# Four shared PSUM rooms, one copy per gather, swaps in eight pieces and a new hand-written order in a gated mix of two long convolutions

## The chip, the cores and the metric

The kernel runs on one core of a Trainium2 chip. The metric is the device time of one execution in microseconds (us). The engines of a core work side by side and each takes its own instructions strictly in their order: TensorE (PE, with its weight loads as PEld), VectorE (DVE), ScalarE (ACT), GpSimd (POOL) and SyncE (SP). DMA transfers are issued by SP, ACT and POOL and run beside the engines. Matmuls write to PSUM, whose eight banks hold 2 KB in each of 128 partitions; a matmul result stays there until DVE or ACT has copied or used it ("evicted").

## The reference

A gate between two long convolutions over L = 2048 positions of D = 448 channels.

```python
# A: diagonal state-space model, kernel K generated from 256 modes per channel
P = exp((dt * (A_re + 1j A_im))[:, :, None] * l)          # D x N x L
K = einsum("dn,dnl,dn->dl", C, P, dt * B).real
a = irfft(rfft(pad(u)) * rfft(pad(K)))[:L] + u * Dskip
# B: shift convolution of four taps, product, long convolution, product
ks = sum(k_padded[t:t+S] * shift_k[:, 3-t] for t in range(4))
kv = ks * v
b = u * (irfft(rfft(pad(kv)) * rfft(pad(ssm_k)))[:S] + kv * ssm_D)
g = sigmoid((u * gate_w).sum(-1, keepdims=True))          # one value for each position
out = g * a + (1 - g) * b                                  # bf16
```

## The kernel before, in words

The 448 channels are four groups of 112 on the partitions, and they are worked through in NQG = 4 steps of NC = 28 channels per group, for B and for A each. A long convolution is a transform done by matmuls. `spread` brings the columns of an input to a tile zs (128 x 32 x 112) through PSUM tiles ps_c. `transform` multiplies it in place, eight of 32 slices to a PSUM tile (the trace calls the tile ps). A second copy with the two halves of the partitions exchanged, zsS, is made by DMA (`swapped`, lines 764 to 768). `products` (line 399) multiplies zs and zsS by the transformed kernel of the convolution. `stage_a` (PSUM ps_a, result U) and `stage_b` (PSUM ps_b) go back, and the epilogues multiply, add and store.

Convolution A needs its kernel K first. `Tables` computes exponentials and sines on ACT (tiles ET, ks_mag, with DVE's phases ks_ph), in four chunks, one for two of the NBLK = 8 blocks of 14 channels per group. `KGen.block` (line 464) builds two tables of powers on DVE (kg_TQ for two blocks, kg_TP for one; kg_P are partial products) and sums over the modes with 448 matmuls into PSUM tile pk, which one copy brings to kg_S. `KGen.gather` (line 511) picks rows with small matmuls into ps_g, a PSUM tile of one bank for each half, and each half is copied to KT (kg_KT) by a strided copy of 448. `block` (line 891) then spreads KT with weights WcK into the tile zsK of the step: for blocks 0 to 5 in four pieces of 4, 4, 4 and 2 columns through one-bank tiles (name ps_g, seen as ps_c in the trace), for the last two in pieces of 8 and 6 through the two-bank rooms.

PSUM is divided at lines 722 and 723: a pool `psum` of three rooms of two banks, in which all of the transforms take turns, and a pool `psk` of single buffers, one bank for pk (line 885) and one for ps_g (line 516 and the spreads of blocks 0 to 5). A matmul that needs a room waits until the room's last content has been evicted.

Evictions go to ACT (`evac`, line 728), or to ACT and DVE by turns (`evac_two`) in the last block.

The front of the run loads the taps shift_k by four small transfers on ACT's queue (line 781), makes from them a diagonal weight tile (in `front`), transposes k by DMA, and convolves it on PE in eight pieces ps_v, which DVE multiplies into vt. Beside this the tables of the first chunk, the weights and the first spreads are made.

The order of the work: the kernel is first recorded, call by call, by the class `Order` (lines 137 to 155). `issue` then replays the calls by the list ORDER (lines 42 to 112: ranges of call numbers), and makes each engine's order the order of that list. So all instructions carry line 149 in the profile, and tiles tell them apart. The steps run

```python
seq = [("B", 0), ("B", 1), ("A", 0), ("B", 2), ("A", 1), None, ("A", 2), ("B", 3)]
for j in range(NBLK - 1):
    step(seq[j], seq[j + 1], j)
```

Each `step` (line 955) holds the spreads and transforms of the next convolution, the stages back of the current one and block j. ORDER interleaves these freely. Behind the loop come the eighth block, the last halves of A's fourth step, the mix and the stores.

Of the kernel before, what the change touches and what calls it, by code (L numbers as in the profile page):

```python
# [136 lines left out]
class Order:  # L137

    def __init__(self, tc):
        self.tc, self.calls = tc, []  # L140
        for e in ("vector", "scalar", "tensor", "gpsimd", "sync"):
            setattr(self, e, Listed(self.calls, getattr(tc.nc, e)))

    def issue(self):
        last, done = {}, 0
        for run in ORDER.split():
# [914 lines left out]
```

## Time and profile before

| | |
|---|---|
| median of 3 runs | 265.6 us (265.38 to 266.52) |
| the profiled execution | 266.88 us |
| its span in the trace | 264.8 us |
| DVE busy | 243.4 us, 506 instructions |
| ACT busy | 226.8 us, 375 instructions |
| PE busy | 213.7 us, 5786 matmuls |
| mean granted TensorE clock | 0.942 of full speed |
| swaps | 16 transfers of 448 KB, 4.4 us from issue to landing |

The page shows busy time by engine, then 40 slices of the span in tenths of busy time, then the chain of work that ended last, then groups of instructions (out<-in, shape, count, busy us, mean ns of one, and the idle time of their engine before them with what ended it). Other views cut the span into windows, or list an engine's instructions in time.

### The profile page before, as it was taken

How to read it: one execution, taken by the hardware profiler on the slowest of the kernel's cores; microseconds unless marked ns; L12 is line 12 of the kernel's file. 1: busy time of each engine (PE TensorE's matmuls, PEld its weight loads, DVE VectorE, ACT ScalarE, POOL GpSimd, SP SyncE). 2: the span in 40 equal slices, each digit the busy share in tenths (PEclk: the TensorE clock that was granted, in tenths of full speed). 3: DMA queues.
4: the chain of work that ended last, by engine and by line, in shares of the span. 5: the costliest groups of instructions: out<-in, count | busy, mean ns of one | idle time of the engine just before them, and what ended most of it. 6: DMA issues, size and time to landing. Idle time of an engine off the chain costs nothing.

```text
span 264.8 us, 12775 instructions
## 1 busy us (share of the span) xinstructions
PE 213.7 (81%) x5786; PEld 194.2 (73%) x5786; DVE 243.4 (92%) x506; ACT 226.8 (86%) x375; POOL 11.8 (4%) x46
## 2 busy tenths in 40 slices
PE   1611849799799999999899898899979998989820
PEld 1501739788688889889788788889969888979720
DVE  6599999899999999999989999989999999989950
ACT  2998789997999999999999999999999999485400
POOL 8000000000000100010100100001000100000000
PEclk9999979999999869999999999999986999999955
DMA  7999669952833702045626230423240360600087
GB/s 153 218 189 192 104 134 203 176 83 32 158 72 72 159 4 57 4 80 119 109 51 141 41 92 2 90 56 73 50 97 2 72 144 2 144 5 2 2 158 122
DMA packets 57077, 24.27 MB, mean 92 GB/s; under 512 B 52032, under 2 KB 54720, under 8 KB 57024
## 3 DMA queue, kind: packets, MB, share of 16 engines
q1 hardware_dynamic: 50752, 19.34, 38.9%
q0 software_dynamic: 1008, 3.21, 6.6%
q10 hardware_dynamic: 5264, 0.92, 2.1%
q8 instruction: 45, 0.74, 1.2%
q14 instruction: 8, 0.07, 0.1%
HBM read 7.95 MB, written 2.87 MB: 41 GB/s over the span
## 4 chain that ended last, share of the span: by engine, by line
DVE 37%; ACT 35%; PE 16%; DMA 4%; issue 3%; SPq 0%; ACTq 0%; DVEq 0%
ACT zs L149 12%; ACT zsK L149 7%; ACT ET L149 6%; DVE kg_P L149 5%; PE ps_v L149 4%; ACT U L149 4%; DVE kg_TQ L149 3%; PE ps_b L149 3%; DVE kg_TP L149 3%; DVE ET L149 3%; PE ps_c L149 3%; DVE zsS L149 3%; DVE vt L149 3%; DVE zs L149 3%; DVE sb_G L149 2%
## 5 line engine op out<-in xcount | busy, mean ns | idle before, releaser
L149 ACT CAST zs<-ps 128x896 bf16<-128x896 f32 x48 | 43.8, 944 | 1.9 <-PE ps L149 1.9
L149 ACT CAST zs<-ps_c 128x1024 bf16<-128x1024 f32 (+1 forms) x48 | 44.0, 976 | 0.5 <-PE ps_c L149 0.4
L149 PEld LDWEIGHTS <-front 128*32 128x32 bf16 (+1 forms) x496 | 19.9, 160 | 27.8 <-issue 17.3
L149 PE MATMUL pk<-kg_TP,kg_TQ 128*32 128x32 bf16 x1792 | 35.4, 241 | 0.9 <-issue 0.7
L149 PEld LDWEIGHTS <-kg_TQ 128*32 128x32 bf16 x1792 | 31.8, 160 | 3.5 <-issue 0.9
L149 PEld LDWEIGHTS <-s_W 128*128 128x128 bf16 x544 | 27.9, 98 | 7.9 <-issue 4.5
L149 PE MATMUL ps_a<-sa_R,zs 128*128 128x128 bf16 x224 | 32.0, 231 | 1.2 <-DVE zs L149 0.7
L149 PE MATMUL ps_b<-U,sb_G 128*128 128x28 bf16 x1024 | 30.8, 178 | 2.6 <-DVE U L149 1.2
L149 ACT CAST U<-ps_a 128x1024 bf16<-128x1024 f32 (+1 forms) x30 | 27.9, 962 | 5.4 <-PE ps_a L149 5.4
L149 PEld LDWEIGHTS <-sb_G 128*128 128x128 bf16 x1024 | 28.7, 98 | 4.7 <-issue 1.9
L149 PE MATMUL ps_v<-front 128*32 128x336 bf16 (+3 forms) x448 | 17.3, 319 | 17.1 <-DVE sb_offs L149 6.9
L149 PE MATMUL ps_a<-sa_R,zsS 128*128 128x128 bf16 x224 | 31.1, 227 | 0.0
L149 PEld LDWEIGHTS <-zs 128*128 128x128 bf16 x224 | 29.0, 150 | 1.9 <-DVE zs L149 0.8
L149 PEld LDWEIGHTS <-zsS 128*128 128x128 bf16 x224 | 29.4, 152 | 0.7 <-DVE zsS L149 0.4
L149 PE MATMUL ps<-zs,s_W 128*128 128x112 bf16 x384 | 27.1, 215 | 3.0 <-ACT zs L149 2.5
L149 DVE TENSOR_TENSOR kg_TP<-kg_TP,ET 128x1792 bf16<-128x1792 bf16 x23 | 24.7, 1083 | 0.5 <-ACT ET L149 0.5
L149 DVE TENSOR_TENSOR kg_TQ<-kg_TQ,ET 128x896 bf16<-128x896 bf16 (+1 forms) x36 | 24.6, 720 | 0.0
L149 ACT ACTIVATE ET<-ks_ph 128x448 bf16<-128x448 int16 x40 | 22.6, 596 | 1.8 <-DVE ks_ph L149 1.7
L149 DVE TENSOR_TENSOR kg_P<-kg_TP,ET 128x1792 bf16<-128x1792 bf16 (+1 forms) x25 | 23.3, 934 | 0.1
L149 ACT ACT_TABLE_LOAD x15 | 19.2, 1283 | 2.0 <-issue 1.8
L149 PE MATMUL ps_c<-Wc,uu 128*64 128x128 bf16 x224 | 18.7, 290 | 0.4 <-ACT zsK L149 0.2
L149 PE MATMUL ps_c<-Wc,vt 128*64 128x128 bf16 x224 | 17.2, 289 | 1.2 <-ACT zs L149 1.2
(101 smaller groups left out, 424.7 us busy)
## 6 DMA issues: line engine op xcount, KB each, us to landing
zsS<-zs SPq DMA_DIRECT2D x16, 448.0 KB, 4.4
kg_TP<-kg_P POOLq DMA_DIRECT2D x7, 448.0 KB, 4.4
vt<-in_B_v_dram SPq DMA_DIRECT2D x4, 448.0 KB, 7.5
skraw<-in_B_ssm_k_dram SPq DMA_DIRECT2D x16, 112.0 KB, 3.4
uu<-in_A_u_dram SPq DMA_DIRECT2D x4, 448.0 KB, 7.1
ks_xf<-xfd SPq DMA_DIRECT2D x3, 336.0 KB, 3.1
out_dram<-vt SPq DMA_DIRECT2D x8, 112.0 KB, 4.4
out_dram<-vt ACTq DMA_DIRECT2D x8, 112.0 KB, 4.6
```

Source lines behind the costliest of these rows:

```text
L149: ins = f(*args, **kw)
```

## The change

- PSUM: `psum` has four rooms of two banks, and `psk` is gone. pk and ps_g are now tiles of the shared rooms. ps_g uses both banks of a room, one for each half.
- The gather's two copies of 448 to KT become one of 896 whose writes are contiguous.
- The spread of KT always goes in pieces of 8 and 6 columns through the shared rooms.
- A swap is eight transfers of 64 partitions by 8 of the 32 slices (112 KB) instead of two of 64 partitions by 32 (448 KB).
- The taps are loaded by two transfers (three groups, then one) instead of four.
- ORDER is new. A list TURNED names 16 recorded copies that change their engine, from ACT to DVE or from DVE to ACT.

The order changes which call stands where on each engine: both transfers of the taps stand ahead of ACT's first work, on SP the load of A_re comes first and that of C_im behind the first of k's transposes, the loads of vt stand behind all four transposes, and the exponentials and sines of the first chunk stand in longer runs, with 3 table loads on ACT in the front instead of 9. On DVE there are 497 instructions instead of 506, and PE has the same number of matmuls.

```diff
--- before.py
+++ after.py
@@ -40,76 +40,82 @@
 NBH = 1
 
 ORDER = (
-    "1 949 553-554 540-541 538-539 557 555-556 962-963 544 964 545 527 559 2 53 60 529 951 533 528 560 18 966 558 7 "
-    "3 11 10 534 12 6 898 916 8 950 61 548 959 0 22 531 36 31-32 34 887 63-65 4 68 67 15 9 952 66 572-576 542 25 914 "
...
-    "6700 6702 6661 6701 6775 6699 6663 "
+    "975 1 961 525-526 557 551 538 0 955 976 558 536 58 970 561 60 552 966 953 962 562 2-3 563 553 540 539 566-567 "
+    "565 527 963 29 23 554 911 964 24 541 30 33 555 537 542 22 61-62 954 956 531 556 967 957 5 11 544 547 900 59 63 "
...
 )
+
+TURNED = (
+    "62 951 1487 1509 2130 2988 4042 4270 6008 6213 6541 6561 6570 6588 6618 6652 "
+)
+
 
 def entry_of(e):
     return 2 + 3 * Q_LEVELS.index(e) if e in Q_LEVELS else EQ_N + 2 + 3 * P_LEVELS.index(e)
@@ -141,7 +147,13 @@
         for e in ("vector", "scalar", "tensor", "gpsimd", "sync"):
             setattr(self, e, Listed(self.calls, getattr(tc.nc, e)))
 
+    def turn(self):
+        for i in map(int, TURNED.split()):
+            f, args, kw = self.calls[i]
+            self.calls[i] = (self.tc.nc.vector.tensor_copy if f.__name__ == "copy" else self.tc.nc.scalar.copy, args, kw)
+
     def issue(self):
+        self.turn()
         last, done = {}, 0
         for run in ORDER.split():
             a, _, b = run.partition("-")
@@ -405,8 +417,8 @@
 
 class KGen:
 
-    def __init__(self, tc, nc, pool, pk, psk, cons, sel_d, d4, EQ, EP):
-        self.tc, self.nc, self.pk, self.psk = tc, nc, pk, psk
+    def __init__(self, tc, nc, pool, psum, cons, sel_d, d4, EQ, EP):
+        self.tc, self.nc, self.psum = tc, nc, psum
         self.pool, self.cons, self.sel_d, self.d4, self.EQ, self.EP = pool, cons, sel_d, d4, EQ, EP
 
     def mult(self, srcs, r, m):
@@ -492,7 +504,7 @@
         back(8, 16)
         back(0, 8)
         at = (j % 2) * M
-        pt = self.pk[:, 0:448].rearrange("p (n b) -> p n b", b=32)
+        pt = self.psum.tile([P, 2, 512], f32, name="pk", tag="ps")[:, 0, 0:448].rearrange("p (n b) -> p n b", b=32)
         for hw in range(CB):
             for hf in range(2):
                 for c in range(2):
@@ -512,9 +524,9 @@
         nc, cons = self.nc, self.cons
         KT = self.pool.tile([P, CB, 64], bf16, name="kg_KT")
         for r in range(8):
-            if r % 4 == 0:
-                pt = self.psk.tile([P, 512], f32, name="ps_g")
-            o = pt[:, (r % 4) * 112:(r % 4) * 112 + 112].rearrange("p (b n) -> p b n", b=8)
+            if r == 0:
+                pt = self.psum.tile([P, 2, 512], f32, name="ps_g", tag="ps")
+            o = pt[:, r // 4, (r % 4) * 112:(r % 4) * 112 + 112].rearrange("p (b n) -> p b n", b=8)
             jobs = []
             for odd in (range(2) if r == 4 else (None,)):
                 st = 1 if odd is None else 2
@@ -547,8 +559,7 @@
                     jobs[jobs.index(x)] = x + (i == 0, i == len(mine) - 1)
             for a0, out, lhsT, rhs, begin, end in jobs:
                 nc.tensor.matmul(out, lhsT=lhsT, rhs=rhs, start=begin, stop=end, tile_position=(0, 32 * a0))
-            if r % 4 == 3:
-                evac(KT[:].rearrange("p n (b r) -> p n b r", r=8)[:, :, :, r - 3:r + 1], pt[:, 0:448].rearrange("p (r b n) -> p n b r", r=4, b=8), r // 4)
+        evac(KT[:].rearrange("p n (b f r) -> p n b f r", b=8, f=2), pt[:, :, 0:448].rearrange("p f (r b n) -> p n b f r", r=4, b=8))
         return KT
 
 
@@ -719,8 +730,7 @@
     wp = ctx.enter_context(tc.tile_pool(name="wp", bufs=1))
     nat = ctx.enter_context(tc.tile_pool(name="nat", bufs=1))
     qp = ctx.enter_context(tc.tile_pool(name="qp", bufs=NBQ))
-    psum = ctx.enter_context(tc.tile_pool(name="psum", bufs=3, space=PSUM))
-    psk = ctx.enter_context(tc.tile_pool(name="psk", bufs=1, space=PSUM))
+    psum = ctx.enter_context(tc.tile_pool(name="psum", bufs=4, space=PSUM))
     dram = ctx.enter_context(tc.tile_pool(name="dram", bufs=1, space=DRAM))
     kgp = ctx.enter_context(tc.tile_pool(name="kgp", bufs=1))
     xfd = dram.tile([P, NBLK, 3, M], f32, name="xfd")
@@ -763,8 +773,9 @@
 
     def swapped(zs):
         swap = qt([P, 32, 4 * NC], "zsS")
-        for r in range(2):
-            nc.sync.dma_start(swap[64 * r:64 * r + 64], zs[64 - 64 * r:128 - 64 * r])
+        for k in range(0, 32, 8):
+            for r in range(2):
+                nc.sync.dma_start(swap[64 * r:64 * r + 64, k:k + 8], zs[64 - 64 * r:128 - 64 * r, k:k + 8])
         return zs, swap
 
     early = kgp.tile([P, 7168], i32, name="early", tag="kg_TQ")
@@ -778,8 +789,9 @@
     cons.rows()
     wraw = cons.carve(8).bitcast(bf16).rearrange("p (g t) -> p g t", t=4)
     top = lambda g: min(112 * g, 320)
-    for g in range(4):
-        nc.scalar.dma_start(wraw[:, g], B_shift_k[top(g):top(g) + P, :])
+    rows = B_shift_k[0:P, :]
+    nc.scalar.dma_start(wraw[:, 0:3], bass.AP(rows.tensor, rows.offset, [[4, P], [448, 3], [1, 4]]))
+    nc.scalar.dma_start(wraw[:, 3], B_shift_k[top(3):top(3) + P, :])
     nc.gpsimd.memset(kt[:, :, 0:16], 0.0)
     for g in range(4):
         nc.sync.dma_start_transpose(kt[:, g, 16:2064].unsqueeze(1), B_k[0][:, top(g):top(g) + P])
@@ -882,9 +894,8 @@
     dj = cons.carve(32)[0:4]
     nc.gpsimd.iota(dj[:], pattern=[[1, 32]], base=0, channel_multiplier=-8)
     V.tensor_scalar(out=sel_d[:], in0=dj[:], scalar1=0.0, scalar2=None, op0=ALU.is_equal)
-    pk = psk.tile([P, 512], f32, name="pk")
-
-    kg = KGen(tc, nc, kgp, pk, psk, cons, sel_d, d4, EQ, EP)
+
+    kg = KGen(tc, nc, kgp, psum, cons, sel_d, d4, EQ, EP)
     KA = [None] * NQG
     XA = [None] * NQG
 
@@ -899,10 +910,7 @@
         KT = kg.gather(j, S, ev)
         at = (j % 2) * CB
         cols = lambda c: KT[:, c, :]
-        if j >= NBLK - 2:
-            spread(nc, psum, WcK, KA[H], cols, [range(0, 8), range(8, 14)], ev, at=at)
-        else:
-            spread(nc, psk, WcK, KA[H], cols, [range(0, 4), range(4, 8), range(8, 12), range(12, 14)], evac, 4, "ps_g", at)
+        spread(nc, psum, WcK, KA[H], cols, [range(0, 8), range(8, 14)], ev, at=at)
 
     def window(t, b0, n, H):
         return t[:, b0:b0 + n, H * NC:(H + 1) * NC]
```

134 rows, old and new, of the table ORDER are left out of this document.

## The prediction

> **What bounds the kernel now.** The page comes first: the span, busy time by engine, the 40 slices and the chain that ended last.
>
> ```profile
> span 264.8 us, 12775 instructions
> PE 213.7 (81%) x5786; PEld 194.2 (73%) x5786; DVE 243.4 (92%) x506; ACT 226.8 (86%) x375; POOL 11.8 (4%) x46
> ...
> DVE  6599999899999999999989999989999999989950
> ACT  2998789997999999999999999999999999485400
> ...
> DVE 37%; ACT 35%; PE 16%; DMA 4%; issue 3%; SPq 0%; ACTq 0%; DVEq 0%
> ```
>
> VectorE (DVE) is busy for 243.4 of 264.8 us, and its gaps lie in the first three slices and the last two. ScalarE (ACT) is full between. The chain changes between the two and belongs to neither. So the question is not which engine is busiest but in which stage an engine still stands idle. The windows view answers that (the span cut into stretches; for each: length, then busy us of PE, PE's weight loads, DVE, ACT, POOL, the granted clock, the DMA share, GB/s).
>
> ```profile
> 0.00:20.00 20.00, 6.09 (x51) 4.62 (x51) 15.20 (x72) 14.57 (x30) 5.65 (x39) 1.00 1.06 187
> 20.00:40.00 20.00, 9.82 (x229) 8.82 (x233) 19.79 (x58) 15.70 (x22) 0.00 (x0) 0.91 0.84 144
> 40.00:48.00 8.00, 7.06 (x232) 6.69 (x226) 6.77 (x18) 7.91 (x16) 0.00 (x0) 1.00 1.12 191
> 48.00:200.00 152.00, 140.71 (x3767) 127.54 (x3761) 149.29 (x291) 148.65 (x250) 5.31 (x6) 0.97 0.40 78
> 200.00:212.40 12.40, 12.31 (x296) 11.28 (x296) 12.29 (x18) 11.96 (x24) 0.85 (x1) 0.86 0.22 40
> 212.40:255.30 42.90, 37.73 (x1238) 35.30 (x1234) 40.06 (x53) 28.05 (x40) 0.00 (x0) 0.95 0.26 58
> 255.30:264.80 9.50, 0.00 (x0) 0.00 (x0) 0.03 (x1) 0.00 (x0) 0.00 (x0) 0.50 0.86 144
> ```
>
> DVE's idle time is length less busy: 4.80 us before 20, 0.21 to 40, 1.23 to 48, only 2.71 in the 152 us to 200, 0.11 to 212.40. That is 9.06 us ahead of 212.40, and 6.24 of them lie before 48. From 212.40 DVE has 40.06 of 42.90 us to do, PE 37.73. The last 9.50 us are stores, with no engine busy. So three things can shorten this kernel: DVE's waits in the front, DVE's work, and the chain of PE and DVE behind 212.40. PE idles 11.29 us between 48 and 200, ACT 3.35: PE has a little room there, ACT hardly any.
>
> **The front.** The timeline of DVE (start, length, operation, and in brackets the idle time before it) and of ACT with its DMA issues:
>
> ```profile
> 4.66 0.30 DVE L149 CAST scratch<-scratch 112x4 f32<-112x4 bf16 x1 [0.35 <-ACT scratch L149]
> ...
> 9.32 1.56 DVE L149 TENSOR_TENSOR front<-scratch 128x1344 bf16<-128x1344 bf16 x1 [3.12 <-DMA scratch<-in_B_shift_k_dram]
> ...
> 47.87 1.09 DVE L149 TENSOR_TENSOR vt<-ps_v,vt 128x896 bf16<-128x896 f32 x1 [1.07 <-PE ps_v L149]
> ```
> ```profile
> 4.42 0.20 ACT L149 ACTIVATE scratch<-ldt 112x4 bf16<-112x4 bf16 x1 [1.36 <-DMA ldt<-in_A_log_dt_dram]
> 4.43 1.35 ACTq L149 DMA_DIRECT2D scratch<-in_B_shift_k_dram  x3
> 6.83 0.54 ACT L149 COPY early<-ps_m 128x448 f32<-128x448 f32 x1 [2.20 <-PE ps_m L149]
> ```
>
> Three of the four tap loads are issued at 4.43, behind an exponential that waits until 4.42 for log_dt. DVE then waits 3.12 us for the last to land. In the new order both tap loads stand ahead of the exponential and of the first table load. Their landing should take what the last one takes now: issued near 5.3, used at 9.32, about 4 us. So issued by about 2 they land near 6. The lists also put about 2.5 us more DVE work ahead of that product. I cost the wait at nothing: **−3.1**. Its cover is those 2.5 us; without it up to about 1 us would remain. The small cast moves to ACT: **−0.35**. The eight products vt<-ps_v idle 1.23 us between 40 and 48. With four rooms instead of three, PE can have one more product's matmuls finished: between 0 and −1.23, I take **−0.9**, since most of it sits before the eighth product.
>
> ACT's table loads: 15 become 9; in the front 9 become 3. Rows of the grouping by form (busy us, mean ns of one | idle before):
>
> ```profile
> L149 ACT ACT_TABLE_LOAD x15 | 19.2, 1283 | 2.0 <-issue 1.8
> ...
> L149 ACT CAST zsK<-ps_c 128x512 bf16<-128x512 f32 x18 | 11.6, 647 | 0.6 <-PE ps_b L149 0.4 <-PE ps_c L149 0.2
> ...
> L149 ACT CAST zsK<-ps 128x896 bf16<-128x896 f32 x12 | 11.2, 975 | 0.5 <-PE ps L149 0.5
> ...
> L149 ACT CAST kg_KT<-ps_g 128x448 bf16<-128x448 f32 x15 | 8.4, 559 | 0.6 <-PE ps_g L149 0.4
> ...
> L149 ACT CAST kg_S<-pk 128x448 bf16<-128x448 f32 x8 | 4.4, 545 | 0.0
> ...
> L149 ACT CAST zsK<-ps_c 128x256 bf16<-128x256 f32 x6 | 2.5, 419 | 0.0
> ...
> L149 ACT CAST zsK<-ps_c 128x1024 bf16<-128x1024 f32 x2 | 2.1, 1034 | 0.5 <-PE ps_c L149 0.5
> ...
> L149 DVE CAST U<-ps_a 128x768 bf16<-128x768 f32 x2 | 1.9, 952 | 0.0
> ...
> L149 DVE COPY kg_TP<-ET 128x224 bf16<-128x224 bf16 x8 | 1.7, 212 | 0.2
> ...
> L149 DVE COPY kg_TQ<-ET 128x448 bf16<-128x448 bf16 x4 | 1.1, 272 | 0.3 <-PE pk L149 0.3
> ...
> L149 DVE CAST zsK<-ps_c 128x768 bf16<-128x768 f32 x1 | 0.9, 949 | 0.0
> ...
> L149 ACT CAST zsK<-ps_c 128x768 bf16<-128x768 f32 x1 | 0.8, 826 | 0.0
> ...
> L149 DVE CAST kg_KT<-ps_g 128x448 bf16<-128x448 f32 x1 | 0.6, 623 | 0.6 <-PE ps_g L149 0.6
> ```
>
> Six loads at 1.283 us are 7.7 us of ACT. This is the largest single number in the change, and I count **0** of it. ACT idles 5.43 + 4.30 us before 40 already. In the new lists its first sines of the second chunk stand behind DVE work that ACT reaches earlier than before, so it waits there instead. DVE, not ACT, is the fuller engine up to 48 (41.76 of 48 us against 38.18).
>
> The Trainium skill ("ScalarE: Activation LUTs", section "What ACT_TABLE_LOAD costs") gives about 1283 ns for the load, which is the row's figure, and a drain of about 1380 ns besides; by it the six would be worth 16.0 us of ACT. The count of 0 stays, since ACT's time there is not what ends last.
>
> **The gather and the spread.** Sixteen evictions of kg_KT (8.4 + 0.6 us) become eight on ACT of twice the size. No row has one with that read order; the nearest of its size is zsK<-ps 128x896 at 0.975, so 7.8. The floor is the 0.545 that half the size costs (kg_S), the ceiling two old copies, 1.12. The spread's 28 evictions (11.6 + 2.5 + 2.1 + 0.8 + 0.9 = 17.9) become 8 x 1.034 + 8 x 0.826 = 14.9. On ACT a part of that comes back: two 768 copies of U move to ACT, and 8 small copies turn. In sum ACT does about 5 us less over the whole run, nearly all of it table loads.
>
> DVE loses U 768 (1.9), zsK 768 (0.9), kg_KT (0.6), five kg_TP<-ET (1.06), one kg_TQ<-ET (0.27) and two small copies (0.6): 5.3. It gains one U copy of 512 (about 0.7). Neighbours overlap by some 0.07 us an instruction (about ten of them). That is **−4.0 us of DVE work**: 243.4 to 239.4. But where it falls matters. Counting DVE's listed work ahead of the last kg_TQ product (the one that ends near 212.40), the new order has only **0.5** less. The other 3.5 come behind it, where DVE is not alone in setting the end.
>
> **The end.** Timeline of PE behind the last kg_TQ product:
>
> ```profile
> 216.12 1.21 PE L149 MATMUL pk<-kg_TP,kg_TQ 128*32 128x32 bf16 x64
> 217.25 0.57 PE L149 MATMUL ps<-zsK,s_W 128*128 128x112 bf16 x8
> 217.75 0.73 PE L149 MATMUL pk<-kg_TP,kg_TQ 128*32 128x32 bf16 x32
> ```
>
> Block 7's 448 pk matmuls cannot begin before that product. In the old list transform matmuls ps<-zsK stand between them, eight to each room, 0.50 us for eight (217.25 to 217.75). In the new list 24 of these stand ahead of the first pk matmul that needs the last kg_TQ. PE's work behind that point falls by 3 x 0.50 = 1.5, the matmuls being otherwise the same. PE has 37.73 of 42.90 us there and takes turns with DVE and ACT, so shorter evictions could give more, and an unlucky turn less: between +1 and −4, I take the PE figure, **−1.5**.
>
> **The swaps.** Each swap was two transfers of 64 partitions, 7168 B a row; it becomes eight of 1792 B.
>
> ```profile
> 64.71 1.18 SPq L149 DMA_DIRECT2D zsS<-zs  x2
> ```
> ```profile
> L149 SPq DMA_DIRECT2D zsS<-zs x16: 461/563/2222, 64.7 to 226.0; - x16
> ...
> DMA to landing us min/median/max: 4.0/4.4/6.7
> ```
> ```profile
> 74.80 2.01 DVE L149 TENSOR_TENSOR zsS<-zsS,zs 128x3584 bf16<-128x3584 bf16 x1
> ```
>
> SP issues one in 0.563 us (median), so eight take 4.5 where two took 1.18. If a piece lands 4.4 us after its issue, the swap ends 7 x 0.56 + 4.4 = 8.3 us after its start; now the second piece ends 0.6 + 4.0 to 6.7. So up to 3.7 us later, or about level. Lower than level is possible if a smaller piece lands sooner: the 112 KB stores and loads on the page's list lie beside bigger ones with no clear order, so I leave that at 0. The first swap started at 64.71 and its product at 74.80: 10.1 us, of which 8.3 are used, and the new list lets it start earlier. I take **0**. Behind the pieces on SP stand skraw and ks_xf loads, needed some 10 us later.
>
> **The sum.** −3.1 − 0.35 − 0.9 − 0.5 − 1.5 = −6.35. The small waits between 48 and 212.40 (2.82 in all) I leave where they are. The profiled execution took 266.88 us (span 264.8 and 2.08 around it); it becomes 260.5. The median of the three runs is 265.6, 1.28 below the profiled one, so 259.2.
>
> **The rivals.**
> *Rooms (slower).* kg_S, kg_KT and both spread evictions of a block now hold one of the four shared rooms, and each of the four stands in ACT's full queue. Before, pk and ps_g had a private bank each, and the spreads of six of the eight blocks used the second. If PE stops for each of them, a block costs 0.545 + 0.975 + 1.034 + 0.826 = 3.38 us of PE. PE's idle time, 11.29 us over seven blocks, absorbs 1.6 of it, and the gain of 6.35 another 0.9. So from 2.5 us a block the sign turns; at the full price it is 7 x (3.38 − 1.6) = +12.5: 271.7. For it speaks that ACT stands idle only 3.35 us in that stretch, so that an eviction rarely goes at once. Against it: the rooms become four where there were three, the old private banks were single and made the chain from pk to zsK serial too, and in the rows above little idle time is put down to kg_KT or kg_S (0.6 us for each form at most).
> *Late front.* Another arrival takes the place of the taps: k's transposed loads or the log_dt chain (ACT's 2.20 us wait for ps_m at 6.83). Then 3 of the 4.35 us of the front stay: 262.2, range 262 to 264.5.
> *Pieces late.* A product waits for a swap. The Trainium skill ("DMA: Bandwidth & Descriptors", section "🔬 Bandwidth") asks for transfers of 1 MiB or more and calls those under 64 KB bound by descriptors; 112 KB lies between, so by it the eight pieces are a loss. In this kernel's rows the loss could be 0 to 3.7 us at each of eight swaps, less their slack; if half of them are short of slack by 1.5, +6: 265.2, range 261 to 268.
> *More.* The waits of 2.82 in the middle go too and the end gives 4: 259.2 − 1.3 − 2.5 = 255.4, range 253.5 to 256.5.
> That the eight pieces don't do what they seem to (they still wait for the whole tile, since the products read all of it) is in the sum, at 0.
>
> **How the numbers follow.** Forecast 259.2, own range 256.5 to 262: 0.62, all faster. More: 0.10, faster. Late front: 0.10, of which 0.02 within 0.5%. Rooms: 0.12, of which 0.01 within. Pieces: 0.06, a third to each sign. A measurement of this kernel can tell about 0.5%, 1.3 us, from no change. Faster 0.62 + 0.10 + 0.08 + 0.02 = 0.82, same 0.05, slower 0.13. The range 254.5 to 265 leaves out the rooms case, the dearer half of the pieces and the edge of the best case, 0.19.
>
> **What would show it.** Right: no DVE wait of over 1 us on the taps, under 3 us of DVE idle before the last vt product, nine table loads and ACT idle before 40 not smaller than the 9.7 of now, 239 to 240 us of DVE busy, the last kg_TQ product about 5 us earlier, no DVE wait on a swap. Wrong: PE idle between 48 and 200 over 20 us, put down to ACT's kg_S, kg_KT or zsK (rooms); a DVE wait on zsS's DMA (pieces); a new front wait of 3 us; or a last kg_TQ product that is 5 us earlier while the end is not.

## The result and the profile after

The changed kernel takes 263.12 us (median of 12 runs, 261.74 to 265.33), the kernel before 267.05 on the same chip (12 runs, 265.38 to 268.82): a ratio of 0.985, interval 0.982 to 0.988, or 3.9 us. Run once more beside the variants below, it gave 261.34 us, ratio 0.982 (0.978 to 0.986), or 4.8 us by the ratio. The forecast was 6.35 us less. The profiled execution took 261.79 us, span 259.5. That is 5.1 us below the profiled one of before, and among the fastest of the twelve.

The page of the changed kernel: span, busy time by engine, the 40 slices of VectorE (DVE) and ScalarE (ACT), and the chain.

```profile
span 259.5 us, 12882 instructions
...
PE 211.7 (82%) x5786; PEld 193.9 (75%) x5786; DVE 238.0 (92%) x495; ACT 221.6 (85%) x360; POOL 13.3 (5%) x46
...
DVE  8999999999799989989989999998999999995940
ACT  2899839999999989999989999999999998849400
...
ACT 19%; PE 13%; DVE 9%; DMA 4%; issue 3%; SPq 0%; ACTq 0%; DVEq 0%
```

DVE's first slice went from 6 to 8 and its second from 5 to 9, so the front filled up. In exchange a 7 and four 8s stand in the middle, where there were two 8s and otherwise 9s. To see what that means in time, cut the span at two marks that both kernels have: the end of the last product vt<-ps_v, and the end of the last product kg_TQ<-kg_TQ,ET. The windows of the kernel before (length, then busy us of PE, weight loads, DVE, ACT, POOL, clock, DMA share, GB/s):

```profile
0.00:48.96 48.96, 23.82 (x528) 20.87 (x529) 42.72 (x147) 38.74 (x67) 5.65 (x39) 0.97 0.98 171
48.96:215.48 166.52, 155.10 (x4076) 140.91 (x4076) 163.26 (x312) 163.13 (x277) 6.17 (x7) 0.96 0.39 75
215.48:254.91 39.43, 34.80 (x1182) 32.47 (x1181) 37.08 (x49) 24.96 (x34) 0.00 (x0) 0.95 0.21 48
```

and of the changed one:

```profile
0.00:42.88 42.88, 25.00 (x536) 22.39 (x536) 41.36 (x145) 31.59 (x66) 7.17 (x39) 0.96 0.98 173
42.88:212.55 169.67, 153.95 (x4104) 140.87 (x4100) 162.99 (x308) 165.15 (x264) 6.16 (x7) 0.98 0.44 82
212.55:249.32 36.77, 32.74 (x1152) 30.65 (x1150) 33.21 (x45) 24.82 (x33) 0.00 (x0) 0.95 0.19 40
```

Front −6.08, middle **+3.15**, end −2.66, and the stores behind it +0.29 (10.18 against 9.89): −5.30, which is the difference of the spans. More was won in the front than forecast, and half of it was given back in the middle. In a second profile (after_again) the same stretches take 43.78, 169.16 and 36.44 us. DVE has no more work in the middle (162.99 against 163.26) but waits 6.68 us instead of 3.26. ACT has 2.02 us more work there. None of that is left over from the front, where ACT did 27.7 us besides its table loads, against 27.2 before. By the forms in the stretch, four copies zsK<-ps that stood behind the last kg_TQ product now stand ahead of it (3.6 us), six turned copies came from DVE (2.8 us), and the larger copies of kg_KT and of the spreads save 3.9 us.

DVE's timeline shows the new waits (start, length, operation, idle time before it and what ended it):

```profile
7.63 1.54 DVE L161 TENSOR_TENSOR front<-scratch 128x1344 bf16<-128x1344 bf16 x1
...
68.00 2.02 DVE L161 TENSOR_TENSOR zs<-zs 128x3584 bf16<-128x3584 bf16 x1 [1.49 <-ACT zs L161]
...
91.97 1.09 DVE L161 TENSOR_TENSOR vt<-ps_b,uu 128x896 bf16<-128x896 f32 x1 [1.02 <-PE ps_b L161]
...
114.86 0.62 DVE L161 TENSOR_TENSOR kg_P<-kg_TP,ET 128x896 bf16<-128x896 bf16 x1 [0.98 <-DMA kg_TP<-kg_P]
...
132.66 1.09 DVE L161 TENSOR_TENSOR kg_TP<-kg_TP,ET 128x1792 bf16<-128x1792 bf16 x1 [0.84 <-DMA kg_TP<-kg_P]
...
238.06 0.62 DVE L161 CAST zsK<-ps 128x448 bf16<-128x448 f32 x1 [2.58 <-PE ps L161]
```

The tap wait of 3.12 us at `front` is gone. In its place stand a product that probably waits for a swap (the row at 68.00 names ACT, but the last piece was issued at 65.42 and zs may not be overwritten before it is read), powers that wait for an accumulating transfer, and a product on ps_b that waits for PE; the last row, an eviction, lies in the end. Three different releasers, each about 1 us, speak against one slow thing.

The forms that the change made (busy us, mean ns | idle before):

```profile
L161 ACT ACT_TABLE_LOAD x9 | 11.5, 1283 | 2.4 <-issue 2.3
L161 ACT CAST zsK<-ps_c 128x1024 bf16<-128x1024 f32 x8 | 8.3, 1042 | 0.2 <-PE ps_c L161 0.2
L161 ACT CAST kg_KT<-ps_g 128x896 bf16<-128x896 f32 x8 | 7.5, 942 | 1.4 <-PE ps_g L161 1.2
L161 ACT CAST zsK<-ps_c 128x768 bf16<-128x768 f32 x8 | 6.6, 829 | 0.4 <-PE ps_a L161 0.4
```

### The profile page after: what moved, and what is told of

It is laid out like the page before. It is cut to its first block, busy times and chain, and to the rows that moved or that the text cites. A ratio compares the mean times of both kernels' runs of the same rounds, so it can differ in the third digit from the quotient of the medians.

```text
span 259.5 us, 12882 instructions
## 1 busy us (share of the span) xinstructions
PE 211.7 (82%) x5786; PEld 193.9 (75%) x5786; DVE 238.0 (92%) x495; ACT 221.6 (85%) x360; POOL 13.3 (5%) x46
## 3 DMA queue, kind: packets, MB, share of 16 engines
HBM read 7.95 MB, written 2.87 MB: 42 GB/s over the span
## 5 line engine op out<-in xcount | busy, mean ns | idle before, releaser
L161 PEld LDWEIGHTS <-front 128*32 128x32 bf16 (+1 forms) x496 | 21.2, 161 | 20.4 <-issue 11.8
L161 PE MATMUL pk<-kg_TP,kg_TQ 128*32 128x32 bf16 x1792 | 34.0, 241 | 2.6 <-DVE kg_TP L161 1.0
L161 PEld LDWEIGHTS <-kg_TQ 128*32 128x32 bf16 x1792 | 31.2, 160 | 5.0 <-DVE kg_TP L161 1.4
L161 PEld LDWEIGHTS <-s_W 128*128 128x128 bf16 x544 | 28.5, 100 | 7.8 <-issue 5.3
L161 ACT CAST U<-ps_a 128x1024 bf16<-128x1024 f32 (+2 forms) x31 | 28.4, 936 | 1.4 <-PE ps_a L161 1.4
L161 PE MATMUL ps_v<-front 128*32 128x224 bf16 (+3 forms) x448 | 18.8, 336 | 9.9 <-DMA front<-in_B_k_dram 2.8
L161 PE MATMUL ps_c<-Wc,vt 128*64 128x128 bf16 x224 | 18.3, 289 | 0.3 <-ACT zs L161 0.3
L161 PE MATMUL ps_c<-Wc,uu 128*64 128x128 bf16 x224 | 17.5, 287 | 0.9 <-ACT U L161 0.6
L161 DVE TENSOR_TENSOR kg_P<-kg_TQ,ET 128x1792 bf16<-128x1792 bf16 (+1 forms) x20 | 17.7, 895 | 0.0
```

The costliest lines, as they stand in the source:

```text
L161: ins = f(*args, **kw)
```

## The experiments

All ratios are to the kernel before, run on the same chip. The changed kernel itself is 0.985 and 0.982 in its two measurements.

### The taps in the old front, and late taps in the new one

```diff
 before_taps: ORDER of before, the other three loads of the taps behind the first (ahead of ACT's exponential)
-  ... 0 22 ... 63 ... 25 ... 24 23 ...
+  ... 0 22 25 24 23 ... 63 ...
```

> The kernel before with its four tap loads in one row ahead of ScalarE's first exponential, nothing else moved. The 3.12 us wait of VectorE on the taps becomes 0 to 1.2 us. If the front passes through to the end: 2 to 3 us faster, ratio 0.988 to 0.993. Rival (the wait only moves, since ScalarE, full from 66 us on, and PE set the middle): below 1 us faster, ratio 0.996 to 1.001, with the idle time of VectorE before 48 us lower by 2 to 3 and later waits higher by as much.

Measured: 266.63 us, ratio 0.998 (0.995 to 1.002). ACT and DVE of this variant:

```profile
1.20 3.22 ACTq L152 DMA_DIRECT2D scratch<-in_B_shift_k_dram  x4
```
```profile
5.98 0.19 DVE L152 CAST scratch<-scratch 112x4 f32<-112x4 bf16 x1 [1.68 <-ACT scratch L152]
...
8.32 1.56 DVE L152 TENSOR_TENSOR front<-scratch 128x1344 bf16<-128x1344 bf16 x1 [1.01 <-DMA scratch<-in_B_shift_k_dram]
...
47.90 1.09 DVE L152 TENSOR_TENSOR vt<-ps_v,vt 128x896 bf16<-128x896 f32 x1 [1.22 <-PE ps_v L152]
```

The four issues take 3.22 us of ACT's queue, so the exponential behind them is late, and DVE waits 1.68 us for that. The taps' product comes 1.0 us earlier (8.32 against 9.32) and the last vt product not at all (47.90 against 47.87): there PE ends the wait. DVE's idle time up to 49.00 is 6.21 us, 6.24 before: the wait moved, and none of it went, not even in the front, where the rival had expected 2 to 3 us less. So in the old order the 3.12 us on the taps cost nothing that this move could bring back. It issues four transfers where the change has two; two in the old order were not tried.

```diff
 after_taps_late: ORDER of after, the load of three groups of taps behind ACT's first copy of ps_m
-  ... 24 541 ... 22 61-62 ... 578 ...
+  ... 24 541 ... 61-62 ... 578 22 ...
```

> The changed kernel with the transfer of three groups of taps issued only behind ScalarE's first copy of ps_m (7.1 us). The taps then land near 11.5 instead of before 7.6, so VectorE waits about 4 us in the front. If the front passes through: 3 to 4 us slower than the changed kernel, ratio to before 0.996 to 1.001. Rival (the middle's waits on transfers and on PE take the shift up): under 1.5 us slower, ratio below 0.991.

Measured: 264.47 us, ratio 0.989 (0.983 to 0.995). DVE waits for the taps again:

```profile
11.52 1.56 DVE L164 TENSOR_TENSOR front<-scratch 128x1344 bf16<-128x1344 bf16 x1 [3.81 <-DMA scratch<-in_B_shift_k_dram]
```

The front is 3.66 us longer (46.54 to the last vt product; 2.76 against the second profile), the middle as long as in the changed kernel, and the profiled span 3.0 us longer (262.5):

```profile
46.54:216.14 169.60, 156.18 (x4100) 143.23 (x4100) 163.20 (x307) 165.08 (x264) 6.16 (x7) 0.96 0.41 78
```

The ratios differ less, by 0.4 to 0.7% (1.0 to 1.8 us), and their intervals overlap; by the ratio it is the rival that was met (below 0.991), though the middle took nothing of the shift up. So in the new order the early taps bring the last vt product forward, and in the old one they didn't. How much of it reaches the end is not settled by these runs.

### The swaps

```diff
 after_swap2: two transfers of 448 KB, where the first two pieces behind the tile's last writer stood
 after_swap4: four of 64 partitions x 16 slices;  after_parts: eight of 16 partitions x 32 slices
-                nc.sync.dma_start(swap[64 * r:64 * r + 64, k:k + 8], zs[64 - 64 * r:128 - 64 * r, k:k + 8])
+            nc.sync.dma_start(swap[64 * r:64 * r + 64], zs[64 - 64 * r:128 - 64 * r])            # after_swap2
+                nc.sync.dma_start(swap[64 * r:64 * r + 64, k:k + 16], zs[64 - 64 * r:128 - 64 * r, k:k + 16])   # after_swap4
+            nc.sync.dma_start(swap[a:a + 16], zs[b:b + 16])                                       # after_parts
 before_swap8: the eight pieces in the kernel before, four where each of its two transfers stood
```

> The changed kernel with each swap as two transfers of 448 KB again, issued where the first two pieces stood (all but a few of the pieces are issued only when the whole tile is written). Theory A (the pieces gave back part of the front's gain): the 1.49 us wait of VectorE before the first product zs (68.00) goes, since two transfers issued at 59.97 land by 59.97 + 6.5 = 66.5, and the 0.32 us wait at 126.93 goes; the accumulating transfers kg_TP<-kg_P land a little sooner. Time 1.5 to 3 us below the changed kernel, ratio to before 0.974 to 0.980. Rival B (the pieces are hidden; the order gives the gain back elsewhere): the time stays within 0.7 us of the changed kernel, ratio 0.982 to 0.988, and VectorE waits somewhere else by the same sum. Rival C (eight pieces land sooner than two): 0.5 to 2 us slower than the changed kernel.

> The kernel before with each swap in eight pieces of 112 KB, in two groups of four where its two transfers stood. By the sum of the prediction the first swap has 10.1 us from issue to use and needs 8.3, so nothing is to be seen: ratio 0.997 to 1.003. Theory A as a general cost of the pieces: products wait at one or more swaps, +1 to +4 us, ratio 1.004 to 1.015.

> The changed kernel once more, for a second profile and to be compared on the chip of its variants. Ratio to before 0.982 to 0.988 as before. Theory F (TensorE now and then runs out of instructions while a swap is under way, stands idle, and the granted clock halves for one window of 3.4 us or two): the half-clock stretches of the clock's record stand behind idle time of PE put down to issue, as those at 88.8 and 123.0 in the first profile, and their number, not the front, makes the difference between single runs. Rival G (the clock dips on its own): the stretches stand anywhere.

> The changed kernel with each swap in eight transfers of 112 KB again, but cut by partitions (16 rows of 7168 B) instead of by slices (64 rows of 1792 B). If it is the pacing of eight issues of 0.6 us that keeps PE's instruction fetches short (theory F with pace): as the changed kernel within 0.8 us, ratio 0.982 to 0.989, idle time of PE put down to issue between 48 and 215 about the 3.9 us of the changed kernel. If it is the length of the rows: as the variant with two transfers, ratio 0.990 to 0.996, and idle time put down to issue near its 9.0 us.

> The changed kernel with each swap in four transfers of 224 KB (64 rows of 3584 B). By theory F the time lies between two and eight pieces: ratio 0.986 to 0.992, PE's idle time for issue between 3.9 and 9.0 us. Rival A (the pieces cost time, the two-transfer variant was slow by chance): at or below the eight-piece kernel, ratio 0.980 to 0.985.

| kernel | a swap | us | ratio (interval) |
|---|---|---|---|
| changed, again | 8 of 64 rows x 1792 B | 261.34 | 0.982 (0.978 to 0.986) |
| after_swap4 | 4 of 64 rows x 3584 B | 262.25 | 0.982 (0.979 to 0.986) |
| after_swap2 | 2 of 64 rows x 7168 B | 265.07 | 0.993 (0.989 to 0.997) |
| after_parts | 8 of 16 rows x 7168 B | 267.54 | 1.000 (0.997 to 1.004) |
| before_swap8 | 8 of 64 rows x 1792 B, old order | 266.49 | 0.997 (0.993 to 1.001) |

Theory A falls: with two transfers the new order is slower, by about 1%. Rival C named that sign, but by an earlier landing, and DVE's wait at the first product zs is no longer with two transfers (1.01 us at 67.67) than with eight (1.49). The number of issues is not it, since the eight transfers cut by partitions are the slowest. What the two slow kinds have in common, in the new order, is rows of 7168 B. after_parts has a second handicap, so it is not a clean test of the row: its transfers land later, and the first product zs waits 2.70 us. In the old order, whose transfers have rows of 7168 B too, the pieces make no difference that can be told.

Where time goes shows on PE, in the profile of after_swap2 (first its timeline, then windows around the second of the two gaps):

```profile
84.13 1.66 PE L161 MATMUL pk<-kg_TP,kg_TQ 128*32 128x32 bf16 x87 [2.26 <-issue]
...
146.56 0.31 PE L161 MATMUL pk<-kg_TP,kg_TQ 128*32 128x32 bf16 x5 [4.11 <-issue]
```
```profile
140.00:145.60 5.60, 2.45 (x127) 2.19 (x119) 5.00 (x16) 4.58 (x8) 0.00 (x0) 1.00 0.66 148
145.60:152.40 6.80, 5.73 (x168) 5.17 (x169) 5.36 (x8) 4.52 (x11) 0.85 (x1) 0.50 0.11 20
```

A swap was issued at 138.66. PE stands idle for 4.11 us with nothing that the profile can name ("issue"), and from 145.65, shortly before PE goes on, the granted clock is 0.50 for 6.8 us. PE's idle time for issue (ps_b, pk, ps, ps_g in the waits view) sums to 9.4 us here, to 5.0 and 4.7 in the two profiles of the changed kernel, to 5.3 in after_swap4 and to 6.4 in after_parts, where near 9 was expected. In the kernel before it is 1.0 us, with rows of 7168 B. So these gaps came with the new order, the longest of them with the long rows, and they don't rank the variants by themselves. The middle stretch shows the result (after_swap2, then after_parts):

```profile
43.02:218.66 175.64, 157.27 (x4100) 144.29 (x4100) 163.35 (x308) 165.76 (x263) 6.17 (x7) 0.92 0.42 80
```
```profile
42.93:217.46 174.53, 156.77 (x4104) 143.44 (x4100) 163.27 (x308) 165.84 (x264) 6.17 (x7) 0.94 0.47 81
```

6.0 and 4.9 us longer than the changed kernel's 169.67, with the same work, at a mean clock of 0.92 and 0.94 instead of 0.98. (The clock alone doesn't set it: the middle of after_taps_late took 169.60 us at 0.96.) That PE waits for its own instructions is argued, not shown: the page lists a queue of kind "instruction" with 45 packets and 0.74 MB, which is 64 B for each of 2 x 5786 matmuls and weight loads, and most of PE's gaps come beside or just behind a swap. Theory F's second half holds only in part: the two half-clock windows of the changed kernel's middle stand, in its first profile, behind PE gaps of 0.98 and 0.84 us, the second of which waited for DVE, not for issue; in the second profile both stand behind gaps for issue (0.79 and 0.88 us). The Trainium skill ("TensorE: Matmul & The Clock Gate", section "🔬 Part 1: The HAM clock gate (the "warmup" mystery)") gives windows of 3413 ns, and the half-clock stretches in the middle of these two kernels are one or two of that length (3.4 and 6.8 us). It has the clock halve after an idle window. Here PE had been busy 0.21 us in the 3.41 us ahead of the half-clock stretch of after_swap2 at 145.65, which agrees nearly, but 2.87 us in those ahead of the one at 88.84 in the changed kernel, which was not an idle window.

### The turned copies

```diff
 after_unturned / after_turn_tail
-    "62 951 1487 1509 2130 2988 4042 4270 6008 6213 6541 6561 6570 6588 6618 6652 "
+    ""
+    "6541 6561 6570 6588 6618 6652 "
```

> The changed kernel without the list of turned copies: 13 copies go back from ScalarE to VectorE, one each of 512 and two of 448 back to the engine of the code as written. VectorE gets about 3 us more work, of which 1.0 stands ahead of the last kg_TQ product. If VectorE's work sets the end: 1 to 3 us slower than the changed kernel, ratio 0.989 to 0.997. Rival (the freed time of VectorE lies beside waits on PE and transfers): within 0.7 us of the changed kernel.

> The changed kernel with only the last six of the 16 turned copies turned (four of zsK and two of U in the last 40 us; five go to ScalarE, one to VectorE). Without any turn the time behind the last kg_TQ product was 39.7 us, with all 36.4 to 36.8. If the end is VectorE's: most of the 1.6% between the two comes back, ratio 0.983 to 0.989. Rival (the copies of kg_TP and kg_TQ earlier matter as much, each being on VectorE's way): 0.990 to 0.996.

Without any turn: 265.93 us, ratio 0.998 (0.995 to 1.000). With the last six alone: 261.39 us, ratio 0.979 (0.975 to 0.983), no slower than with all 16. So the list is worth 1.3 to 1.6%, and the six copies of the end are, as far as can be told, all of it. It also means that everything else in the change together, without the list, comes to 0.2%; the gains of the parts don't add up, since the pieces alone cost 1% when taken away. The last stretch without turns, to set beside 36.77 us with 33.21 of DVE:

```profile
213.37:253.07 39.70, 33.29 (x1150) 30.93 (x1150) 36.21 (x49) 22.06 (x29) 0.00 (x0) 0.93 0.18 37
```

3.00 us less DVE work there is 2.93 us less time (3.26 against the second profile), while PE's work differs by 0.55. Against the kernel before, this variant has 1.51 us less PE work in the end (33.29 against 34.80), and the end is no shorter (39.70 against 39.43). The end is DVE's.

### The waits in the middle

```diff
 after_mended: 13 calls of DVE moved in ORDER to just ahead of the call that waits, for instance
-  ... 3611 ... 2971 ...
+  ... 2971 3611 ...
 after_mended4: the same on after_swap4
```

> The changed kernel with 14 of VectorE's instructions moved ahead of the eight instructions that waited between 48 and 182 us in both profiles of it (products behind swaps, powers behind the accumulating transfers, evictions behind PE); other engines keep their order, and no work is left out. The eight waits are 5.1 to 5.6 us in the two profiles, the moved work is about 6 us. If VectorE's new waits in the middle are what the forecast lost: 2 to 4 us faster than the changed kernel, ratio to before 0.968 to 0.976, VectorE's idle time between 43 and 212 down from 6.7 to 2 to 3.5. Rival (ScalarE and PE set the middle, VectorE's waits only show it): within 1 us of the changed kernel, ratio 0.980 to 0.987, the idle time moved elsewhere.

> The same with swaps in four transfers of 224 KB. The first product's wait was 0.3 us there instead of 1.1 to 1.5, but PE's waits for issue were longer (1.8, 1.8 and 1.1). Theory: within 0.7 us of the mended kernel with eight pieces, ratio 0.968 to 0.977. If long rows cost more where VectorE waits less: 0.5 to 1.5 us slower than that one.

Measured: 262.21 us, ratio 0.982 (0.977 to 0.986), and 264.31 us, ratio 0.985 (0.980 to 0.991); the two can't be told apart. The rival was right about the time. The middle of after_mended, and two of DVE's rows in it:

```profile
42.95:214.20 171.25, 155.21 (x4100) 142.41 (x4100) 163.67 (x308) 165.39 (x264) 6.17 (x7) 0.97 0.43 82
```
```profile
128.28 0.28 DVE L164 TENSOR_SCALAR ks_ph<-ks_xf 128x224 int32<-128x224 f32 x1 [1.44 <-ACT ET L164]
...
133.81 0.39 DVE L164 TENSOR_TENSOR ET<-ET,ks_mag 128x448 bf16<-128x448 bf16 x1 [0.65 <-ACT ET L164]
```

The waits for transfers at 114.86 and 132.66 are gone, and waits for ACT stand in their place. DVE's idle time in the stretch is 7.6 us, not less.

```diff
 after_less_act
+        for i in (every fourth of the 48 calls ET<-ks_xf): self.calls[i] = []
```

> The changed kernel with 12 of the 48 exponentials ET<-ks_xf left out (one in four of each chunk's sixteen; the entries of the chunk before stay in their place), all of them on ScalarE between 48 and 200 us: by the row of the changed kernel (48 in 17.0 us) 4.2 us less work there, none less on VectorE or TensorE. Theory S (the middle, from the last vt product to the last kg_TQ product, is ScalarE's: 165.2 of 169.2 to 169.7 us busy, 2.0 more than before the change): that stretch becomes 165 to 167, ratio to before 0.967 to 0.975. Rival V (VectorE's list sets it, 163.0 busy): the stretch stays within 1 us, ratio 0.980 to 0.986.

Measured: 260.12 us, ratio 0.974 (0.970 to 0.979).

```profile
42.90:211.71 168.81, 154.49 (x4104) 141.55 (x4100) 162.84 (x307) 163.14 (x253) 6.15 (x7) 0.96 0.43 81
```

The work taken away is 2.0 us in the stretch and 3.0 in the run, not 4.2 (neighbours on ACT overlap more than the row let me think). The stretch is 0.35 to 0.86 us shorter than in the two profiles of the changed kernel, which is rival V's sign; the ratio is 0.8 to 1.1% lower, which is theory S's. ACT is busy 163.14 us here, as in the kernel before (163.13), and the stretch is still 2.3 us longer than there. So theory S holds in part at most: ACT has a share in the middle's length, and what else sets it was not found.

## Why the prediction was right, and where it was not

**Direction and range** were right; the gain was 3.9 and 4.8 us where 6.35 was forecast. That the sum came so near is in part luck: the front and the end each gave more than forecast, by 1.7 and 1.2 us in the profiles, and their main terms stood for the wrong thing, while the middle took 3.15 us back.

**The step that failed** is the one that let the front's gain pass through: "The small waits between 48 and 212.40 (2.82 in all) I leave where they are." The middle grew by 3.15 us (2.64 in the second profile). Both engines were nearly full there before, ACT busy for 163.13 of 166.52 us and DVE for 163.26. The prediction counted ACT's work only over the whole run, as 5 us less; by stage it is 7.15 less in the front and 2.02 more in the middle, where ACT had 3.39 us free. DVE's idle time there rose by 3.42 us, with waits for swaps, accumulating transfers and PE.

The earlier start is not what made it longer: with the front 3.66 us longer (after_taps_late) the middle took 169.60 us, as in the changed kernel. Filling DVE's waits (after_mended) gave nothing, and less work for ACT gave 0.35 to 0.86 us. On PE the idle time put down to issue is 3.9 us in the stretch instead of 1.0, but after_taps_late and after_unturned have 2.2 and 1.8 us of it and the same middle to within half a microsecond (169.60 and 169.17). So the cause lies in the changed kernel's middle itself, not in when it starts. Its order, its rooms and its larger evictions were not taken apart there, and mending the lists of several engines at once was not tried: the cause stays open.

**The front** gained more than its sum, −4.35 forecast and −6.08 measured (−5.18 in the second profile), with DVE's idle time in it down from 6.24 to 1.52 us. But its main term was not what the sum said. Earlier taps alone bring the last vt product nowhere (before_taps). In the new order late taps give 3.66 of the 6.08 us back (after_taps_late); what else in the front's order did the rest was not taken apart. I had read the 3.12 us as a price, though other waits stood behind it: in before_taps the wait behind the exponential took over 1.3 us, 1.0 stayed on the taps, and the rest went to waits for ACT and PE.

**The table loads at 0** were not tested. ACT does 7.15 us less up to the first mark, and its idle time there goes from 10.22 to 11.29 us. No run puts the six loads back, so part of the front's gain may be theirs. The drain of 1380 ns that the Trainium skill gives in the section named in the prediction ("ScalarE: Activation LUTs", "What ACT_TABLE_LOAD costs") is not seen here: nine loads cost 1283 ns each, with 0.1 us of idle time ahead of all but one of them.

**DVE's work**: −4.0 forecast, −5.4 by the pages (243.4 to 238.0); up to the last kg_TQ product −1.6 instead of −0.5 (205.98 to 204.35 by the first two windows). I also took the wrong instruction for that product: the last one ends at 215.48, not near 212.40. No term of the sum hangs on that. DVE's 3.5 us behind the product, which I counted at nothing because DVE is "not alone in setting the end", were 3.87 and were the term that counted.

**The end**: −1.5 forecast by PE's work, −2.66 measured. It is DVE's work that counts there: after_unturned has the forecast's 1.5 us less PE work and no shorter end. So the six turned copies were the gain, and the 24 transform matmuls were not needed for it.

**The swaps at 0**: in the new order they are a gain of about 1%, in the old one nothing. The rival of late pieces came out the other way: in the new order the variants with rows of 7168 B are 0.8 to 1.9% slower (0.993 and 1.000 against 0.985 and 0.982). So did the Trainium skill's rule for large transfers ("DMA: Bandwidth & Descriptors", section "🔬 Bandwidth"), as the prediction applied it; the table that the rule stands under is for loads from HBM, and a swap stays within SBUF. A piece lands 2.8 us after its issue, not 4.4.

**The rooms** as a rival did not come: PE's idle time from 48.96 or 42.88 to the last kg_TQ product is 11.4 before and 15.7 us after, but 3.9 of the latter is for issue (1.0 before) and 4.0 for DVE (0.5 before), and none of its gaps of over half a microsecond from 60 to 215 is put down to kg_S or kg_KT; one of 0.92 is put down to zsK, where there were two before (0.51 and 1.12). The rooms alone were not tried.

**The signs** named for "right" came in part: nine table loads, no wait on the taps, 1.52 us of DVE idle time before the last vt product. But DVE's busy time was 238.0 us instead of 239 to 240, the last kg_TQ product came 2.9 us earlier instead of 5, and DVE did wait on a swap. One sum is off: the rival *More* takes 1.3 us for waits that it gives as 2.82; with all of them its time would be 253.9.

## What to carry to other kernels

Before you count a wait as a gain, look for the wait behind it that would take it over. Count every nearly full engine's work by stage, not over the run: here ACT's 5 us less were 7 less in the front and 2 more in the stretch where it was 98% busy, and the front's 6 us came through as 3. Work taken off the engine that alone has the end, as six copies here, is worth nearly its full time. To learn whether an earlier start is lost in the next stage, delay it again: here the middle kept its length. When cutting a transfer, vary the length of a row and the number of transfers apart: here eight transfers with long rows were no faster than two, and the long rows went with the slow kernels.

## What the runs showed of the hardware

In the new order with swaps of 7168 B a row (after_swap2) PE idles for up to 4.11 us with no wait to name, and the half-clock stretches at its three longest gaps last 3.4 or 6.8 us; the old order has rows as long and 1.0 us of such idle time in all, so the rows alone don't do it. The same work in the same stretch took 175.64 us at a mean clock of 0.92 and 169.67 at 0.98. A piece of 112 KB lands 2.8 us (median) after its issue when it has 64 rows of 1792 B (2.4 in the second profile), and 3.4 with 16 rows of 7168 B:

```profile
zsS<-zs SPq DMA_DIRECT2D x64, 112.0 KB, 2.8
```
```profile
zsS<-zs SPq DMA_DIRECT2D x64, 112.0 KB, 3.4
```

Single runs of the changed kernel differ by 3.6 us; the profiles differ in the number and place of the half-clock stretches, but the mean clock of a run does not tell its time (261.75 us at 0.940, 265.33 at 0.953).
